# Scores of the first stretch over 128 rows: two k heads in one tile, each head's q beside zeros

## The chip, the core and the metric

The kernel runs on one core of a Trainium2 chip. Its engines are TensorE (PE; its weight loads stand apart as PEld), VectorE (DVE), ScalarE (ACT), GpSimd (POOL) and SyncE (SP, which issues every transfer of this kernel). Each engine takes its instructions strictly in its own order. The metric is the device time of one execution in microseconds, the median of several.

## What is computed

Attention over the 32 largest scores of each query, for 4 batches of 8 heads with 576 positions and head size 64, and then two MLPs on the 2304 tokens of 512 numbers.

```python
scores = scale * np.matmul(q, k.transpose(0, 1, 3, 2))
kth = np.partition(scores, -top_k, axis=-1)[..., -top_k:-top_k + 1]      # top_k = 32
scores = np.where(scores >= kth, scores, -1000000000.0)
attn = np.exp(scores - np.max(scores, axis=-1, keepdims=True))
attn = attn / (np.sum(attn, axis=-1, keepdims=True) + 1e-09)
x = np.matmul(attn, v)                    # then (tokens, 512)
h = x @ w_in;  x = (h - np.tanh(h)) @ w_out              # first MLP
h = x @ w_in2; out = np.where(h > 0.0, h, np.exp(np.minimum(h, 0.0)) - 1.0) @ w_out2
```

## The kernel before

The queries are cut into six chunks of 384. In each chunk the heads go in four pairs, and a pair's rows of scores form groups of at most three tiles of 128 queries by 576 keys. There are 48 groups, eight to a chunk. In chunk 0 (groups 0 to 7) and chunk 2 (groups 16 to 23) a group is one head's 384 queries.

A loop over "ticks" writes the program, four ticks to a group: loads at the start of a tick, then the top-32 search (`topk_steps`) with parts of MLP steps between its operations, then transposes of the exponentials (`transposed`), then `norm`, `attend` and `finish_pair`. The framework's scheduler then settles the order on each engine, with the tick order and a few priorities as its guide. So an edit in one place can move instructions elsewhere.

The search is DVE's: for each tile four times MAX8 (line 351: the eight largest) and three or four times MATCH_REPLACE8 (line 365: overwrite these) or, at the end, a masking operation (line 372, or ACT at lines 367 and 368).

Scores come in two ways. Most groups split q and k in high and low parts (`split_qk`) and multiply over 128 rows (lines 328 and 329). The groups of chunk 0 ("whole") and of chunk 2 ("parked") multiply unsplit float32 over the 64 rows of a head (line 326); the program's one matmul there is two MATMUL instructions in the profile. Each result of 128 by 288 is copied from PSUM by ACT (line 330). Whole scores (tile `ps`, three PSUM banks) go straight to the search. Parked ones (tile `pp`, two PSUM banks) are computed during the first stretch at low priority, copied to `sp`, stored to DRAM as `sd` (line 306), and read back much later. The first stretch is thus chunk 0's attention with chunk 2's scores beside it: 8 whole and 8 parked units, six score matmuls of the program each.

Loads of q and k are at lines 263 and 270. A whole or parked unit loads its head's q (64 rows by 384) into `qraw` and its head's k (64 rows by 576) into `kraw`, both in rows 0 to 63. There are two buffers each for whole units (tags `qraw`, `kraw`) and one each for parked units (tags `qp`, `kp`).

In the same stretch the MLP weights are prepared (`prepare`): a load of 512 KB (`wr`, line 166, three buffers), two ACT operations (lines 175 and 176, or 176 and 180), a product on POOL (line 178), a combination on DVE (line 181, output `wf`, two buffers), a split in high and low on ACT and POOL (lines 140 and 141, output `wp`), and a store to DRAM (line 186). Later chunks load the prepared weights (`wt`). MLP steps are `first` (matmul `h`, line 500), `gate`, and `second` (matmul `acc`, line 536). `attend` is the product with v (matmul `av`, line 415), `transposed` the transposes (`pt`, line 393).

Of the kernel before, what the change touches and what calls it, by code (L numbers as in the profile page):

```python
# [8 lines left out]
F32 = mybir.dt.float32  # L9
# [10 lines left out]
P = 128  # L20
B, H, S, D = 4, 8, 576, 64
# [4 lines left out]
HS = S // 2  # L26
# [51 lines left out]
QR_BUFS = 2  # L78
KR_BUFS = 2
# [19 lines left out]
NU = 384  # L99
# [8 lines left out]
def tile_topk_attention_two_mlps(  # L108
# [9 lines left out]
    nc = tc.nc  # L118

    def pool(name, bufs, space=None):  # L120
        kw = {} if space is None else {"space": space}
        return ctx.enter_context(tc.tile_pool(name=name, bufs=bufs, **kw))

    const = pool("const", 1)
    sb = pool("sb", 2)
# [10 lines left out]
    def f(ap):  # L136
        return ap.bitcast(F32)

    def split(hi, lo, src):
        nc.scalar.activation(hi, src, copy)  # L140
        nc.gpsimd.tensor_sub(lo, src, f(hi))  # L141

    def bank(tag, name, bufs):
        return ps.tile([P, 512], F32, tag=tag, name=name, bufs=bufs)
# [63 lines left out]
    for ci, size in enumerate(SIZES):  # L208
        for p in range(NPAIR):
            row = []  # L210
            c0 = 0
            for b, q0, n in CHUNKS[ci]:
                for heads in ([[0], [1]] if n >= 256 else [[0, 1]]):
                    u = Unit()
# [10 lines left out]
            cuts, k = [], 0  # L225
# [28 lines left out]
    def parked(u):  # L254

        return u.g.at in PARK

    def load_q(u):
        u.qraw = sb.tile([P, NU], F32, tag="qp" if parked(u) else "qraw", name=f"qraw{u.id}", bufs=1 if parked(u) else QR_BUFS)
        src = qT[u.b, 2 * u.p + u.heads[0] : 2 * u.p + u.heads[-1] + 1, :, u.q0 : u.q0 + u.n].rearrange("h d s -> d h s")  # L260
        nq = u.n * len(u.heads)
        for half in range(1 if u.whole or parked(u) else 2):
            nc.sync.dma_start(u.qraw[half * D : half * D + D, :nq].rearrange("d (h s) -> d h s", s=u.n), src)

    def load_k(u):
        u.kraw = {}
        for h in u.heads:
            u.kraw[h] = sb.tile([P, S], F32, tag="kp" if parked(u) else "kraw", name=f"kraw{u.id}_{h}", bufs=1 if parked(u) else KR_BUFS)
            for half in range(1 if u.whole or parked(u) else 2):
                nc.sync.dma_start(u.kraw[h][half * D : half * D + D], kT[u.b, 2 * u.p + h])  # L270

    def split_qk(u):

        if u.whole or parked(u):
            return
        u.kh, u.kl = {}, {}
        nq = u.n * len(u.heads)
        u.qs = sb.tile([P, NU], F32R, tag="qs", name=f"qs{u.id}", bufs=QS_BUFS)[:, :nq]
        nc.scalar.activation(u.qs, u.qraw[:, :nq], copy)
        nc.gpsimd.tensor_sub(u.qs[D:P], u.qraw[D:P, :nq], f(u.qs[D:P]))  # L280
        for h in u.heads:
            k = sb.tile([P, 2, S], F32R, tag="kk", name=f"kk{u.id}_{h}", bufs=KK_BUFS)
            u.kh[h], u.kl[h] = k[:, 0], k[:, 1]
            split(u.kh[h], u.kl[h], u.kraw[h])
# [7 lines left out]
    def segments(u, t):  # L292

        out = []
        for i, h in enumerate(u.heads):
            lo, hi = max(0, i * u.n - t * P), min(P, (i + 1) * u.n - t * P)
            if lo < hi:
                out.append((lo, hi, h, t * P + lo - i * u.n))
        return out

    def park(u, t):

        s = sb.tile([P, S], F32, tag="sp", name=f"sp{u.id}_{t}", bufs=PARK_BUFS)
        products(u, t, s, True)
        u.parked[t] = dr.tile([P, S], F32, tag=f"sd{u.id}_{t}", name=f"sd{u.id}_{t}")
        nc.sync.dma_start(u.parked[t], s)

    def scores(u, t):
        if t == 0:
            u.s = []  # L310
        s = sb.tile([P, S], F32, tag="s", name=f"s{u.id}_{t}", bufs=S_BUFS)
        u.s.append(s)
        if parked(u):
            nc.sync.dma_start(s, u.parked[t])
        else:
            products(u, t, s, u.whole)

    def products(u, t, s, whole):

        for half in range(2):  # L320
            cs = slice(half * HS, half * HS + HS)
            for lo, hi, h, _ in segments(u, t):
                pt = bank("h", f"pp{u.id}_{t}_{half}_{h}", 2) if parked(u) else bank("at", f"ps{u.id}_{t}_{half}_{h}", 3)
                qc = slice(t * P, t * P + P)
                if whole:
                    nc.tensor.matmul(pt[:, :HS], u.qraw[0:D, qc], u.kraw[h][0:D, cs], start=True, stop=True)  # L326
                else:
                    nc.tensor.matmul(pt[:, :HS], u.qs[:, qc], u.kh[h][:, cs], start=True, stop=False)  # L328
                    nc.tensor.matmul(pt[:, :HS], u.qs[:, qc], u.kl[h][:, cs], start=False, stop=True)  # L329
                nc.scalar.activation(s[lo:hi, cs], pt[lo:hi, :HS], copy)  # L330
# [283 lines left out]
    for g in groups:  # L614
        t0 = 4 * g.at
        for u in g.units:
            lead = 6 if u.whole else 8
            if parked(u):
                at = PARK_AT + PARK_STEP * parks[0]
                parks[0] += 1  # L620
                on(before, int(at) - 3, lambda u=u: (load_q(u), load_k(u)))
                for t in range(u.k):
                    on(ends, int(at + t * PARK_STEP / 3), lambda u=u, t=t: later(park, u, t))
            else:
                on(before, max(-6, t0 - lead) if u.whole else t0 - lead, lambda u=u: (load_q(u), load_k(u)))
                on(before, t0 - 5, lambda u=u: split_qk(u))
            on(before, t0 + (1 if hurried(u) else 3), lambda u=u: load_v(u))
        for blk in range(NB):
            if not hurried(g.units[-1]):
                on(late, t0 + 4 + (1 if g.units[0].ci == 1 else 0) + (0 if quick(g.units[-1]) else blk // 3), lambda g=g, blk=blk: transposed(g, blk))  # L630
        for j, (u, t) in enumerate(g.tiles):
            on(mid, t0 - 4 + j, lambda u=u, t=t: scores(u, t))
        for u in g.units:
            if hurried(u):
                continue
            if u.last:
                on(ends, t0 + (5 if quick(u) else 7), lambda u=u: norm(u.ci, u.p, u))
                on(ends, t0 + (5 if quick(u) else 7), lambda u=u: attend(u))
                on(ends, t0 + (5 if quick(u) else 7), lambda u=u: finish_pair(u))
# [93 lines left out]
```

## Time and profile before

| | us |
|---|---|
| median of 3 runs (1241.11, 1245.57, 1245.80) | 1245.57 |
| the profiled execution | 1243.85 |
| its span, from the first to the last instruction | 1242.1 |

| engine | busy us | share of the span |
|---|---|---|
| PE | 1191.5 | 96% |
| DVE | 975.6 | 79% |
| ACT | 773.8 | 62% |
| POOL | 583.8 | 47% |

The shares are means over stages that differ, so the rows below are taken by stretch. The profile lists the granted clock of PE as a share of full speed: 1.00 is 2.4 GHz, 0.50 is 1.2 GHz, and a number between is a mix of the two over the stretch. The share of the 16 DMA engines can come out a little above 1. A bracket at the end of a timeline row gives how long the engine sat idle before it, and what ended that.

### The profile page before, as it was taken

The numbers are of one execution on the slowest core, as the hardware profiler recorded it, in microseconds if no ns is written. First come the engines' busy times: TensorE is split into PE (matmuls) and PEld (weight loads), VectorE is DVE, ScalarE is ACT, GpSimd is POOL, SyncE is SP. The second block draws the span as 40 slices with busy tenths as digits, with TensorE's granted clock in tenths as the row PEclk, the third lists the DMA queues.
The fourth block names the chain that finished last, engine by engine and source line by source line (L and its number), as shares of the span: only waits on it lengthen the run. The fifth ranks groups of instructions, "written<-read, shape, count | busy, mean of one in ns | idle before, by whom it ended". The sixth has DMA issues, their size and how long they took to land.

```text
span 1242.1 us, 19800 instructions
## 1 busy us (share of the span) xinstructions
PE 1191.5 (96%) x6424; PEld 999.4 (80%) x6424; DVE 975.6 (79%) x1951; ACT 773.8 (62%) x1700; POOL 583.8 (47%) x613
## 2 busy tenths in 40 slices
PE   7799889999989999999999999999999999999998
PEld 4455569888768888988988989988988988889887
DVE  7989999999999999869889768899789997100111
ACT  5989988788786445556566565666555564432333
POOL 4676549978984232334433344544334413233221
PEclk9995689999999999999999999999999999999999
DMA  8999627897979875767756778768777655687672
GB/s 260 341 317 313 228 85 252 299 323 238 317 261 356 326 244 176 245 207 251 241 193 204 235 231 263 239 189 244 220 245 242 198 163 175 198 284 252 218 253 78
DMA packets 103080, 298.32 MB, mean 240 GB/s; under 512 B 12609, under 2 KB 27969, under 8 KB 102977
## 3 DMA queue, kind: packets, MB, share of 16 engines
q1 hardware_dynamic: 102976, 297.06, 72.9%
q8 instruction: 51, 0.84, 0.3%
q14 instruction: 53, 0.43, 0.1%
HBM read 251.66 MB, written 45.35 MB: 239 GB/s over the span
## 4 chain that ended last, share of the span: by engine, by line
PE 74%; DVE 8%; ACT 6%; DMA 6%; POOL 3%; issue 2%; SPq 1%; ACTq 0%; POOLq 0%; DVEq 0%
PE acc L536 28%; PE h L500 28%; PE av L415 5%; PE pt L393 5%; DMA wr<-in_w_dram 4%; DVE vm L351 3%; DVE w L365 2%; PE ps L328 2%; PE pp L326 2%; PE ps L329 2%; DMA kraw<-in_kT_dram 1%; DVE wf L181 1%; PE ps L326 1%; POOL wr L178 1%; ACT ph L394 1%
## 5 line engine op out<-in xcount | busy, mean ns | idle before, releaser
L141 POOL TENSOR_TENSOR gl<-g,gh 128x384 fp32r<-128x384 f32 x192 | 206.5, 1076 | 364.9 <-ACT gh L140 321.9
L351 DVE MAX8 vm<-w 128x8 f32<-128x576 f32 x432 | 316.0, 748 | 3.4
L536 PE MATMUL acc<-wt,gh 128*128 128x512 f32 x1008 | 268.3, 398 | 0.3 <-ACT gh L140 0.3
L536 PEld LDWEIGHTS acc<-wt,gh 128*128 128x128 f32 x1008 | 185.5, 188 | 34.5 <-issue 3.9
L365 DVE MATCH_REPLACE8 w<-vm,w 128x576 f32<-128x576 f32 x288 | 212.8, 740 | 0.0
L140 ACT ACTIVATE gh<-g 128x384 fp32r<-128x384 f32 x192 | 100.8, 525 | 82.9 <-DVE g L514 47.5
L500 PE MATMUL h<-zh,wt 128*128 128x384 f32 (+2 forms) x768 | 146.6, 326 | 2.3 <-ACT zh L555 1.9
L536 PE MATMUL acc<-wt,gl 128*128 128x512 f32 x504 | 148.2, 398 | 0.0
L514 DVE SCALAR_TENSOR_TENSOR g<-t,h 128x384 f32<-128x384 f32 x96 | 52.0, 542 | 118.7 <-ACT t L506 118.7
L351 DVE MAX8 vm<-s 128x8 f32<-128x576 f32 x144 | 107.2, 749 | 46.8 <-ACT s L330 46.5
L500 PE MATMUL h<-xh,wt 128*128 128x384 f32 x672 | 143.0, 340 | 0.0
L393 PE MATMUL pt<-ident,e 128*116 128x128 f32 (+1 forms) x720 | 119.0, 293 | 18.5 <-ACT s L330 6.1
L500 PEld LDWEIGHTS h<-zh,wt 128*128 128x128 f32 x768 | 124.9, 190 | 9.2 <-ACT zh L555 3.1
L330 ACT ACTIVATE s<-ps 128x288 f32<-128x288 f32 (+1 forms) x272 | 106.3, 412 | 41.1 <-PE ps L329 33.1
L394 ACT ACTIVATE ph<-pt 116x384 f32<-116x384 f32 (+1 forms) x240 | 110.6, 498 | 31.1 <-PE pt L393 30.0
L393 PEld LDWEIGHTS pt<-ident,e 128*116 128x116 f32 (+1 forms) x720 | 90.2, 143 | 45.6 <-ACT s L330 10.0
L500 PEld LDWEIGHTS h<-xh,wt 128*128 128x128 f32 x672 | 117.7, 188 | 6.9 <-issue 0.6
L372 DVE SCALAR_TENSOR_TENSOR e<-s,vm,e 128x576 f32<-128x576 f32 x115 | 113.3, 990 | 1.4 <-ACT e L355 0.6
L178 POOL TENSOR_TENSOR wr<-wr,tiny 128x512 f16<-128x512 f32 x64 | 92.1, 1443 | 41.9 <-ACT wr L176 38.7
L505 ACT ACTIVATE t<-h 128x384 f32<-128x384 f32 x96 | 46.7, 488 | 103.0 <-PE h L500 102.8
L536 PEld LDWEIGHTS acc<-wt,gl 128*128 128x128 f32 x504 | 92.7, 188 | 18.4 <-issue 0.6
L365 DVE MATCH_REPLACE8 w<-vm,s 128x576 f32<-128x576 f32 x144 | 106.6, 740 | 0.0
(83 smaller groups left out, 2029.9 us busy)
## 6 DMA issues: line engine op xcount, KB each, us to landing
wt<-w SPq DMA_DIRECT2D x336, 512.0 KB, 4.4
wr<-in_w_dram SPq DMA_DIRECT2D x64, 512.0 KB, 5.9
w<-wp SPq DMA_DIRECT2D x64, 512.0 KB, 4.9
kraw<-in_kT_dram SPq DMA_DIRECT2D x112, 144.0 KB, 4.3
vraw<-in_vL_dram SPq DMA_DIRECT2D x64, 160.0 KB, 2.9
qraw<-in_qT_dram SPq DMA_DIRECT2D x80, 96.0 KB, 3.9
sd<-sp SPq DMA_DIRECT2D x24, 288.0 KB, 4.7
s<-sd SPq DMA_DIRECT2D x24, 288.0 KB, 4.9
```

The lines of the kernel that those rows point to most:

```text
L140: nc.scalar.activation(hi, src, copy)
L141: nc.gpsimd.tensor_sub(lo, src, f(hi))
L178: nc.gpsimd.tensor_mul(top, scaled, tiny)
L330: nc.scalar.activation(s[lo:hi, cs], pt[lo:hi, :HS], copy)
L351: nc.vector.max(g.vm[:, j, min(r, 1)], u.s[t] if r == 0 else g.w[j])
L365: nc.vector.match_replace(g.w[j], v, u.s[t] if r == 0 else g.w[j], FILL)
L372: nc.vector.scalar_tensor_tensor(u.e[t], u.s[t], v[:, 7:8], u.e[t], op0=ALU.is_ge, op1=ALU.mult, accum_out=g.sum[:, j : j + 1])
L393: nc.tensor.transpose(pt[:kn, j * P : j * P + P], v.e[t][:, k0 : k0 + kn], ident)
L394: nc.scalar.activation(g.ph[:kn, blk, :nq], pt[:kn, :nq], copy)
L415: nc.tensor.matmul(banks[c0][h * D : h * D + D, : v.n], v.vraw[h][:kn, blk], v.g.ph[:kn, blk, cs], start=(blk == order[0]), stop=(blk == o ...
L500: nc.tensor.matmul(h[:, cs], wv[:, wi, kt], xs[:, kt, cs], start=(a == 0), stop=(a == len(jobs) - 1))
L536: nc.tensor.matmul(acc[ci, m][t], gx[:, t * P : t * P + P], wt[:, wi], start=(ft == 0 and k == 0), stop=(ft == NF - 1 and k == 2),)
```

## The change

For whole and parked units (`wide(u)`), a pair's k is one tile of 128 rows, head 0 in rows 0 to 63 and head 1 in rows 64 to 127. Both halves are loaded when head 0's unit comes up; head 1's unit loads no k. Each head's q keeps a tile of its own. It is loaded into the head's half of the rows, and POOL fills the other half with zeros. The score matmul then runs over all 128 rows, where the zeros take the other head out. Only group 0 keeps 64 rows. The tags and the number of buffers stay, so the two `kraw` buffers now hold two pairs instead of two heads.

```diff
+    pair_k = {}
+
+    def wide(u):
+
+        return u.whole or parked(u)
+
     def load_q(u):
-        u.qraw = sb.tile([P, NU], F32, tag="qp" if parked(u) else "qraw", name=f"qraw{u.id}", bufs=1 if parked(u) else QR_BUFS)
+        if wide(u):
+            h = u.heads[0]
+            tag, bufs = ("qp", 1) if parked(u) else ("qraw", QR_BUFS)
+            u.qraw = sb.tile([P, NU], F32, tag=tag, name=f"qw{u.id}", bufs=bufs)
+            nc.gpsimd.memset(u.qraw[(1 - h) * D : (2 - h) * D, : u.n], 0.0)
+            nc.sync.dma_start(u.qraw[h * D : h * D + D, : u.n], qT[u.b, 2 * u.p + h, :, u.q0 : u.q0 + u.n])
+            return
...
     def load_k(u):
+        if wide(u):
+            if u.heads[0] == 0:
+                tag, bufs = ("kp", 1) if parked(u) else ("kraw", KR_BUFS)
+                k = pair_k[u.ci, u.p] = sb.tile([P, S], F32, tag=tag, name=f"kw{u.id}", bufs=bufs)
+                for h in range(2):
+                    nc.sync.dma_start(k[h * D : h * D + D], kT[u.b, 2 * u.p + h])
+            u.kraw = pair_k[u.ci, u.p]
+            return
...
                 if whole:
-                    nc.tensor.matmul(pt[:, :HS], u.qraw[0:D, qc], u.kraw[h][0:D, cs], start=True, stop=True)
+                    rows = slice(0, D if u.g.at == 0 else P)
+                    nc.tensor.matmul(pt[:, :HS], u.qraw[rows, qc], u.kraw[rows, cs], start=True, stop=True)
```

The scheduler answers with another order on every engine, up to about row 840 of DVE's 1406; behind that DVE's and ACT's orders are the same as before. Two places matter below. In the names, `_0_1_192_1` is a parked unit (pair 0, batch 1, query 192 on, head 1), `_1_0_0_0` a whole one (pair 1, batch 0, head 0). The changed file's lines are 21 or 22 further down behind the edit (141, 166, 178 and 186 keep theirs).

POOL, from the first weights to the third, before:

```order
L178 TENSOR_TENSOR wr_13_0_505<-wr_13_0_505,tiny 128x512
L141 TENSOR_TENSOR wp_12_0_386<-wf_12_0_380,wp_12_0_386 128x512
L353 TENSOR_SCALAR mb_0_0_0_0_0_0_167<-vm_0_0_0_0_0_0_166 128x3
L141 TENSOR_TENSOR wp_12_1_398<-wf_12_1_392,wp_12_1_398 128x512
L178 TENSOR_TENSOR wr_13_1_517<-wr_13_1_517,tiny 128x512
```

and now, with what each waits for:

```order
L178 TENSOR_TENSOR wr_13_0_511<-wr_13_0_511,tiny 128x512 [waits DMAHW6_49,Activation_49]
L269 MEMSET qw_0_1_192_1_244 64x384 [waits PE_49]
L269 MEMSET qw_1_0_0_1_327 64x384 [waits PE_49]
L141 TENSOR_TENSOR wp_12_0_391<-wf_12_0_385,wp_12_0_391 128x512 [waits Activation_49]
L141 TENSOR_TENSOR wp_12_1_403<-wf_12_1_397,wp_12_1_403 128x512 [waits Activation_49]
L178 TENSOR_TENSOR wr_13_1_523<-wr_13_1_523,tiny 128x512 [waits DMAHW3_49,Activation_49]
```

Two fills, each waiting for PE to be done with the tile's last user, now stand ahead of `wp_12_0`. There are 16 such fills on POOL.

SP, the queue of transfers some 20 us into the run, before:

```order
L186 DMA w_12_1_98<-wp_12_1_398 128x1024
L166 DMA wr_14_1_640<-in_w_dram 128x512
L263 DMA qraw_0_1_192_1_239<-in_qT_dram 64x384
L270 DMA kraw_0_1_192_1_1_241<-in_kT_dram 64x576
L186 DMA w_13_0_99<-wp_13_0_513 128x1024
L306 DMA sd_0_1_192_0_2_347<-sp_0_1_192_0_2_340 128x576
L263 DMA qraw_1_0_0_1_323<-in_qT_dram 64x384
L270 DMA kraw_1_0_0_1_1_325<-in_kT_dram 64x576
```

and now:

```order
L270 DMA qw_0_1_192_1_244<-in_qT_dram 64x384
L270 DMA qw_1_0_0_1_327<-in_qT_dram 64x384
L284 DMA kw_2_0_0_0_490<-in_kT_dram 64x576 x2
L166 DMA wr_14_0_634<-in_w_dram 128x512
L186 DMA w_12_0_97<-wp_12_0_391 128x1024
L327 DMA sd_0_1_192_0_2_350<-sp_0_1_192_0_2_343 128x576
```

The loads of the second heads' k are gone here. The k that is loaded at this place is that of pair 2, a whole pair ahead of its use.

## Rows read from the trace of the kernel before

**Rows 1.** Busy time by stretch: PE, PEld, DVE, ACT, POOL, granted clock, DMA share.

```profile
0.00:40.00 40.00, 26.64 (x52) 16.15 (x52) 31.30 (x63) 25.07 (x53) 19.69 (x25) 1.00 0.86 291
40.00:160.00 120.00, 110.31 (x321) 63.35 (x322) 109.31 (x212) 110.00 (x255) 76.35 (x86) 0.76 0.84 286
160.00:380.00 220.00, 201.68 (x1199) 170.67 (x1198) 219.07 (x419) 183.03 (x392) 182.31 (x175) 0.96 0.77 256
380.00:520.00 140.00, 139.01 (x776) 119.97 (x775) 140.00 (x301) 70.20 (x152) 42.81 (x50) 1.00 0.78 272
520.00:1242.00 722.00, 713.88 (x4082) 629.27 (x4080) 475.94 (x960) 385.46 (x851) 262.60 (x277) 1.00 0.69 219
```

**Rows 2.** DVE's waits from 0 to 160: total us, times, longest.

```profile
DVE vm L351 <- ACT s L330: 11.4, 7, 5.7
DVE wf L181 <- POOL wr L178: 5.4, 4, 2.0
DVE wf L181 <- POOL wp L141: 0.4, 1, 0.4
```

**Rows 3.** The same view of windows, other stretches of the start.

```profile
10.00:20.00 10.00, 10.00 (x22) 6.84 (x22) 9.09 (x20) 7.68 (x18) 6.57 (x6) 1.00 0.82 275
20.00:120.00 100.00, 84.70 (x215) 47.47 (x215) 90.12 (x177) 88.84 (x204) 66.55 (x74) 0.84 0.95 328
70.00:80.00 10.00, 10.00 (x30) 5.40 (x31) 7.78 (x16) 10.00 (x24) 5.23 (x7) 1.00 0.92 292
90.00:120.00 30.00, 29.48 (x75) 16.91 (x75) 28.65 (x57) 28.18 (x68) 19.07 (x23) 0.50 0.95 328
```

**Rows 4.** Timeline of PE: start, us, line, tile, weights' rows*columns, moving rows x columns.

```profile
13.10 2.12 PE L326 MATMUL pp<-kraw,qraw 64*128 64x288 f32 x4
15.02 3.08 PE L326 MATMUL ps<-kraw,qraw 64*128 64x288 f32 x6
...
41.61 1.65 PE L393 MATMUL pt<-ident,e 128*116 128x128 f32 x6 [0.39 <-ACT e L368]
...
63.14 2.25 PE L326 MATMUL pp<-kraw,qraw 64*128 64x288 f32 x4 [1.85 <-DMA kraw<-in_kT_dram]
...
76.71 5.56 PE L415 MATMUL av<-ph,vraw 116*64 116x384 f32 x20
82.20 1.24 PE L326 MATMUL pp<-kraw,qraw 64*128 64x288 f32 x4
83.28 1.13 PE L326 MATMUL ps<-kraw,qraw 64*128 64x288 f32 x4
...
106.40 2.12 PE L326 MATMUL pp<-kraw,qraw 64*128 64x288 f32 x4
...
124.74 1.20 PE L393 MATMUL pt<-ident,e 128*116 128x128 f32 x9
```

**Rows 5.** Timeline of DVE: three waits for weights.

```profile
30.46 0.69 DVE L181 SCALAR_TENSOR_TENSOR wf<-sc,wr 128x512 uint32<-128x512 uint32 x1 [1.14 <-POOL wr L178]
68.46 0.69 DVE L181 SCALAR_TENSOR_TENSOR wf<-sc,wr 128x512 uint32<-128x512 uint32 x1 [1.36 <-POOL wr L178]
79.14 0.69 DVE L181 SCALAR_TENSOR_TENSOR wf<-sc,wr 128x512 uint32<-128x512 uint32 x1 [1.99 <-POOL wr L178]
```

**Rows 6.** Timeline of ACT: what stands behind the first two of these.

```profile
27.78 0.64 ACT L175 ACTIVATE sc<-wr 128x512 f32<-128x512 f32 x1 [1.89 <-DMA wr<-in_w_dram]
64.47 0.41 ACT L330 ACTIVATE sp<-pp 128x288 f32<-128x288 f32 x1 [0.95 <-PE pp L326]
```

**Rows 7.** Timeline of POOL: the nearest operations to a fill of 64x384.

```profile
0.71 0.20 POOL masks.py:197 MEMSET ident<- 128x128 f32 x1 [0.29 <-POOLq L721]
145.87 1.00 POOL L280 TENSOR_TENSOR qs<-qraw,qs 64x384 fp32r<-64x384 f32 x1 [1.10 <-ACT qs L279]
```

**Rows 8.** SP's waits from 0 to 160 before q loads: total us, times, longest.

```profile
SPq L263 <- PE pp L326: 5.1, 4, 2.3
SPq L263 <- PE ps L326: 4.5, 4, 1.4
```

More of the change, by code (lines that the diff above doesn't have):

```diff
@@ L256, in parked @@
         return u.g.at in PARK
+    pair_k = {}
+    def wide(u):
+        return u.whole or parked(u)
     def load_q(u):
-        u.qraw = sb.tile([P, NU], F32, tag="qp" if parked(u) else "qraw", name=f"qraw{u.id}", bufs=1 if parked(u) else QR_BUFS)
+        if wide(u):
[5 more added lines that the diff above has]
+            return
+        u.qraw = sb.tile([P, NU], F32, tag="qraw", name=f"qraw{u.id}", bufs=QR_BUFS)
         src = qT[u.b, 2 * u.p + u.heads[0] : 2 * u.p + u.heads[-1] + 1, :, u.q0 : u.q0 + u.n].rearrange("h d s -> d h s")
         nq = u.n * len(u.heads)
-        for half in range(1 if u.whole or parked(u) else 2):
+        for half in range(2):
             nc.sync.dma_start(u.qraw[half * D : half * D + D, :nq].rearrange("d (h s) -> d h s", s=u.n), src)
     def load_k(u):
+        if wide(u):
[6 more added lines that the diff above has]
+            return
         u.kraw = {}
         for h in u.heads:
-            u.kraw[h] = sb.tile([P, S], F32, tag="kp" if parked(u) else "kraw", name=f"kraw{u.id}_{h}", bufs=1 if parked(u) else KR_BUFS)
-            for half in range(1 if u.whole or parked(u) else 2):
+            u.kraw[h] = sb.tile([P, S], F32, tag="kraw", name=f"kraw{u.id}_{h}", bufs=KR_BUFS)
+            for half in range(2):
                 nc.sync.dma_start(u.kraw[h][half * D : half * D + D], kT[u.b, 2 * u.p + h])
     def split_qk(u):
-        if u.whole or parked(u):
+        if wide(u):
             return
```

## The prediction

> **What bounds the kernel now.** I read the windows by stretch first. From 380 us to the end PE is busy 852.89 of 862 us [rows 1]: whatever brings the point at 380 forward brings the end forward. From 160 to 380 DVE is busy 219.07 of 220 us while PE idles 18 [rows 1]: here the search and the preparation of weights on DVE set the pace, and since DVE never waits, the stretch has a fixed length. So the end moves by as much as DVE reaches 160 us earlier or later, and a gain in the first 160 us can be no more than DVE's idle time there. That time is small. From 40 to 160 DVE is idle 10.7 of 120 us [rows 1]. The list of its waits says for what [rows 2]: 11.4 us in seven waits for scores, of which 5.7 is the unavoidable first one, 5.4 us in four waits for POOL's product of a weight, and 0.4 us for a buffer. Behind the first wait this is 5.7 + 5.4 + 0.4 = 11.5 us, the ceiling of any gain. ACT is as full from 40 to 160 (110.0 of 120 us), and from 20 to 120 the DMA engines are 0.95 busy [rows 1, 3].
>
> PE looks busy in this stretch, and the timeline shows why. Four 64-row instructions follow one another in 15.02 - 13.10 = 1.92 us or, as a single row, 2.12 us: about 0.5 us each. At 82.20, right behind 20 `av` instructions, the next four start 1.08 us later, 0.27 us each [rows 4]. The same work takes half as long. The same holds for the transposes, 0.275 us each at 41.61 and 0.13 at 124.74 [rows 4]. From 90 to 120 the granted clock is 0.50, the lower level of 1.2 GHz [rows 3]. For the first 80 us the profile lists 1.00, but the durations there are those of the 0.50 stretch, so I go by the durations: PE runs the first stretch at the lower level, apart from some microseconds behind each `av`.
>
> What lifts it? PE was busy 10.00 of 10 us from 10 to 20 [rows 3] with 64-row matmuls, and the next ones were no faster. Then 5.56 us of `av`, which fill 116 rows, halved the time of what followed, and by 106.40 the 64-row matmuls were back at 0.5 us [rows 4]. The transposes at 124.74 stand behind the second `av`, with the same effect. That speaks for the rows filled, not for the time busy. The changed scores fill 128.
>
> **The change part by part.**
>
> *Score matmuls over 128 rows.* Their count stays: 16 units of 12 instructions, 192 in all. A 128-row one isn't in the trace in this form. The bounds are 0.27 us (64 rows, after `av`) and 0.5 us (64 rows, elsewhere) [rows 4]. The transposes, with 128 rows moving, take 0.13 us for 128 columns, 288/128 of which is 0.29 us [rows 4], so rows in themselves cost nothing. I take 0.27 us: the clock rises some microseconds behind group 0's twelve 64-row instructions and stays up. PE then has 192 x 0.23 = 44 us less to do in a stretch where DVE's idle time is the only thing that counts.
>
> The Trainium skill, page "TensorE: Matmul & The Clock Gate", Part 3 (packing small matmuls), says that a matmul over few rows takes the same time as one over all of them, and that the gain is to be had by placing two of them in different rows so that they run side by side. By that rule zeros beside a head's q give nothing and the change would end where rival B does; rows 4 agree about a single matmul at a given clock, and the rule leaves out what the clock does.
>
> *DVE's waits for scores*, 5.7 us in six places [rows 2]. Each is PE, then ACT's copy, then MAX8. With score matmuls at half the time, PE runs ahead as far as its three banks go. I take all 5.7.
>
> *DVE's waits for weights*, 5.4 us in four places [rows 2]. The one of 1.14 us at 30.46 goes back to a 512 KB load that landed at 27.78 [rows 5, 6]; PE has no part in it. The one of 1.36 at 68.46 stands behind ACT's copy at 64.47, which waited for `pp`, which waited at 63.14 for a head's k [rows 4 to 6]; with half the k waits gone and PE fast I take it, 1.4. The one of 1.99 at 79.14 has ACT ahead of it, busy 10.00 of 10 us from 70 to 80 [rows 3], and stays. The fourth (0.9) is at the start, and it stays too. So 1.4 of 5.4.
>
> *Fills on POOL*, 16 of 64x384. The trace has none; a fill of 128x128 took 0.20 us, and a product of 64x384 with two inputs 1.00 [rows 7]. By elements per row the first gives 0.6 us, which I take; 16 are 9.6 us (3.2 to 16). POOL has room, 76.35 of 120 us busy [rows 1]. But DVE does wait for POOL, 5.8 us [rows 2] for the 96 us that POOL works up to 160 [rows 1]; in that proportion 9.6 us more cost 0.6. Two of the fills now stand right ahead of the split that frees `wf` for DVE, so I take twice that, 1.2, as a loss, with ends 0 (every fill in a gap of POOL's) and 9.6 (rival C, where a fill also holds POOL while it waits for PE).
>
> *Loads.* The count stays, 16 of q and 16 of k. The two halves of k go ahead of the first weights, and the first DVE operation on weights comes some places later in DVE's order, which covers that, so I put zero; if it didn't, I would expect no more than the longest wait for a weight, 2.0 us [rows 2]. A whole pair's k comes a pair ahead, where before PE waited for a head's k with a single buffer. What that is worth is in the waits above.
>
> *The order.* The scheduler moves things up to about row 840 of DVE's 1406, by a few places either way. In the stretches where DVE or PE never idles, the order has little to give. I put zero and 2 us either way.
>
> Sum: 5.7 + 1.4 - 1.2 = 5.9 us gained. A check from transfers: at a share of 0.95 from 20 to 120 us, these 100 us cannot shrink by more than about 5 us before the engines are full [rows 3]; the slack behind 120 and the start have to give the rest. That fits the sum, and it says not to expect the ceiling of 11.5. From the profiled execution, 1243.85 - 5.9 = 1238.0 us. That execution is 1.7 us under the median of 1245.57, which is within the spread of those runs; I leave the sum where it is: 1238 us, 0.6% under the median.
>
> **The rivals.**
>
> *A: the clock rises, and ACT or the DMA engines take PE's place.* ACT is 92% busy and the transfers at 0.95 [rows 1, 3]; DVE's waits turn from "scores late" to "weights late". Only half of the 5.7 us for scores and none for weights is then won, less 1.2 for fills: 2.85 - 1.2, about 1.6 us, 1242.2. For it: 4 us of the weights' waits already have nothing to do with PE. Against it: the six waits for scores are 0.95 us on the mean, and ACT's copy takes 0.41 of it [rows 2, 6].
>
> *B: the clock doesn't rise.* Matmuls stay at 0.5 us: it was the dense `av` and not its rows, or zeros do not count as rows filled, or with PE at half its load the clock falls back between the bursts. Then k ahead of time wins the 1.4, and the fills cost 1.2: no change, 1243.7.
>
> *C: slower; POOL stands still behind its fills.* A fill cannot start before PE has read the tile's last content, and all of POOL's products and splits of weights stand behind it in order, then DVE's `wf`, which has two buffers. SP had this same wait before q loads: 5.1 + 4.5 = 9.6 us in eight places [rows 8]. If POOL inherits it and DVE meets it in full, with nothing won because PE stays slow, the time is 1243.85 + 9.6 + 1.2 = about 1255. It decides from the point where PE frees a tile later than POOL comes to the fill; a fast PE makes it rare.
>
> **How the numbers follow.** The forecast (clock up, waits for scores gone) has 0.50, A 0.24, B 0.14, C 0.12. The forecast's own range is from 1243.85 - 11.5 - 2 = 1230 to 1241. Adding A and B reaches to 1246, and the spread of the runs by another microsecond; C's far part is left out. Range 1230 to 1247. About 0.5% (6.2 us of 1245.57, so under 1239.3) is what a measurement of this kernel can tell from no change. Most of the forecast's case lies below that, A mostly not: faster 0.50, same 0.39, slower 0.11.
>
> **What would show it.** In the changed profile the 192 score instructions at about 0.27 us from some 15 us on, and transposes at 0.13; a granted clock near 1 from 90 to 120; DVE's waits for scores behind the first one under 2 us in total; DVE idle from 40 to 160 at about half of 10.7; the fills at about 0.6 us. The point from which PE never idles would come some 6 us sooner than 380. Wrong would be: score instructions still at 0.5 us (B), POOL's products waiting for PE by way of a fill (C), or waits for scores gone while DVE waits for weights as long as before or longer (A).

## The result: slower by 1.2%

The changed kernel takes 1259.84 us (median of 6 runs, 1256.26 to 1263.02) and the kernel before, on the same chip, 1245.43 (1240.52 to 1246.00). The ratio is 1.0116, with a 95% interval of 1.0098 to 1.0135. The forecast was 1238 with a range up to 1247. The profiled execution of the changed kernel takes 1256.26 us; its span is 1254.3.

The windows answer to [rows 1] (PE, PEld, DVE, ACT, POOL, granted clock, DMA share, GB/s):

```profile
0.00:40.00 40.00, 24.04 (x56) 14.92 (x56) 30.13 (x60) 22.49 (x49) 18.45 (x29) 0.82 0.78 259
40.00:160.00 120.00, 86.82 (x333) 50.94 (x332) 112.32 (x221) 114.68 (x266) 86.20 (x100) 0.80 0.86 297
160.00:380.00 220.00, 198.83 (x1164) 169.07 (x1164) 218.11 (x410) 176.56 (x376) 178.39 (x170) 0.95 0.74 250
380.00:520.00 140.00, 133.10 (x730) 113.94 (x731) 137.66 (x297) 69.89 (x150) 45.02 (x51) 0.98 0.74 260
520.00:1254.00 734.00, 726.11 (x4144) 639.77 (x4142) 482.48 (x967) 390.36 (x861) 266.10 (x281) 1.00 0.69 219
```

From 40 to 160 PE has 23 us less to do, and DVE does 3 us more work than before. The start has therefore become faster. The loss is behind it: from 160 to 520 PE is busy 331.9 us where it was 340.7, and executes 81 instructions fewer. DVE is as full as before from 160 to 380 (218.1 of 220, 1.8 us of waits), and all the same the end comes later. PE is the one that waits more. From 160 to 520 its waits ahead of the MLP's products (tiles `h` and `acc`) come to 16.4 us in 15 places, where they were 7.3 us in six. The largest before (total us, times, longest):

```profile
PE acc L536 <- ACT gh L140: 2.4, 2, 2.0
PE h L500 <- DVE g L519: 2.3, 1, 2.3
...
PE h L500 <- DVE g L514: 1.5, 1, 1.5
```

and in the changed kernel:

```profile
PE acc L558 <- ACT gh L140: 4.7, 2, 2.6
...
PE h L522 <- DVE g L536: 3.2, 2, 2.8
...
PE acc L558 <- POOL gl L141: 1.9, 3, 0.9
```

Here `g` is the gated hidden tile of an MLP step, and `gh` and `gl` are its high and low parts.

To see where, I followed one instruction of the MLP steps: the n-th `gh` on ACT. The first stands at 188.0 us in the profile of before. In the changed kernel it comes 3.7 us earlier, the 7th (215) is 2.3 late, the 10th (238) level, the 19th (302) 4.7 late, the 31st (380) 6.3 and the 49th (484) 13.5; from the 73rd (605) to the end the shift is 12 us. It wavers on the way and grows. The search doesn't follow: the first MAX8 of its 43 tiles from 183 to 490 us is between 3.0 us earlier and 5.0 later.

DVE's waits from 0 to 160 answer to [rows 2] (total us, times, longest):

```profile
DVE vm L373 <- ACT s L352: 10.0, 7, 5.6
DVE wf L181 <- POOL wp L141: 2.0, 1, 2.0
DVE wf L181 <- ACT wr L180: 1.5, 2, 1.1
DVE wf L181 <- POOL wr L178: 1.4, 2, 0.9
```

PE's timeline answers to [rows 4] (start, us, tile; the bracket is the idle time before the row, with what ended it):

```profile
14.87 1.53 PE L348 MATMUL pp<-kw,qw 128*128 128x288 f32 x4
...
17.69 1.13 PE L348 MATMUL pp<-kw,qw 128*128 128x288 f32 x4
...
22.59 3.81 PE L348 MATMUL pp<-kw,qw 128*128 128x288 f32 x8 [2.32 <-DMA qw<-in_qT_dram]
...
100.75 2.26 PE L348 MATMUL pp<-kw,qw 128*128 128x288 f32 x4 [2.03 <-DMA kw<-in_kT_dram]
...
107.16 1.13 PE L348 MATMUL pp<-kw,qw 128*128 128x288 f32 x4
```

The clock does rise: four score instructions take 1.13 us at 17.69, 0.28 each. Behind an idle PE they are back at 0.48 to 0.57 us (22.59, 100.75). The granted clock from 90 to 120 us is 0.85, where it was 0.50 [rows 3]:

```profile
90.00:120.00 30.00, 20.74 (x88) 12.99 (x88) 28.17 (x59) 28.07 (x68) 20.82 (x27) 0.85 0.95 318
```

### The profile page after: what moved, and what is told of

The parts are those of the page before. It is cut to its first block, busy times and chain, and to the rows that moved or that the text cites. A ratio compares the mean times of both kernels' runs of the same rounds, so it can differ in the third digit from the quotient of the medians.

```text
span 1254.3 us, 19826 instructions
## 1 busy us (share of the span) xinstructions
PE 1168.9 (93%) x6424; PEld 988.6 (79%) x6424; DVE 980.7 (78%) x1951; ACT 774.0 (62%) x1700; POOL 594.2 (47%) x629
## 4 chain that ended last, share of the span: by engine, by line
PE 69%; ACT 10%; DVE 10%; DMA 5%; issue 3%; POOL 3%; SPq 1%; ACTq 0%; POOLq 0%; DVEq 0%
PE h L522 28%; PE acc L558 28%; PE av L437 5%; PE pt L415 4%; DVE vm L373 4%; DVE w L387 3%; DMA wr<-in_w_dram 3%; PE ps L350 2%; DVE wf L181 2%; PE ps L351 2%; ACT s L352 1%; ACT wr L176 1%; ACT ph L416 1%; ACT e L390 1%; ACT e L377 1%
## 5 line engine op out<-in xcount | busy, mean ns | idle before, releaser
L522 PEld LDWEIGHTS h<-zh,wt 128*128 128x128 f32 x768 | 126.1, 191 | 10.7 <-ACT zh L577 3.9
L415 PE MATMUL pt<-ident,e 128*116 128x128 f32 (+1 forms) x720 | 116.4, 286 | 17.4 <-ACT e L390 8.1
L415 PEld LDWEIGHTS pt<-ident,e 128*116 128x116 f32 (+1 forms) x720 | 88.2, 140 | 39.9 <-ACT e L390 12.8
L527 ACT ACTIVATE t<-h 128x384 f32<-128x384 f32 x96 | 46.8, 489 | 109.0 <-PE h L522 109.0
L525 ACT ACTIVATE t<-h 128x384 f32<-128x384 f32 x96 | 47.1, 492 | 102.7 <-PE h L522 102.2
```

What stands on the lines that cost most here:

```text
L415: nc.tensor.transpose(pt[:kn, j * P : j * P + P], v.e[t][:, k0 : k0 + kn], ident)
L522: nc.tensor.matmul(h[:, cs], wv[:, wi, kt], xs[:, kt, cs], start=(a == 0), stop=(a == len(jobs) - 1))
```

## Two theories, and the crossing that tells them apart

Theory 1: the loss is the order in which the scheduler now puts the instructions of all engines behind 160 us. Theory 2: it is the edit's own work (fills that wait for PE, weights that come late, a clock that falls). Order and work can be crossed. A helper keeps each engine's instructions in a given order by edges that need no wait; the n-th instruction of the program text on an engine is the same in both kernels, apart from the loads of q and k and the fills, which are found by name.

**x1**: the changed work in the order of before.

```diff
+def pin(tc, order):
+    # keep each engine's instructions in a given order (edges without a wait)
...
+    for engine, tokens in order.items():
...
+        line = [plain[t] if isinstance(t, int) else known[t] for t in tokens if isinstance(t, int) or t in known]
+        for a, b in zip(line, line[1:]):
+            tc.add_manual_dep(b, a.name, info, reason="order")
...
         tile_topk_attention_two_mlps(tc, *args)
+        pin(tc, ORDER)
```

`ORDER` lists every engine as in the kernel before.

> The changed kernel (scores over 128 rows, fills, a pair's k in one tile) with the instructions of every engine kept in the order of the kernel before; only the fills lie where the scheduler puts them, and the second k half of a pair is issued right behind the first. Theory 1, the order: the loss lies in the order that the scheduler found for the work between 160 and 640 us, not in the edit's own work, so this kernel gains what the score stage gains, 1238 to 1246 us. Theory 2, the edit's own work (fills that wait for PE, later weights, the clock that falls back in PE's gaps): it stays at 1254 to 1262 us whatever the order.

**x2**: products over 64 rows in the order of the changed kernel, with a pair's k still in one tile.

```diff
-            nc.gpsimd.memset(u.qraw[(1 - h) * D : (2 - h) * D, : u.n], 0.0)
...
-                    rows = slice(0, D if u.g.at == 0 else P)
+                    rows = slice(h * D, h * D + D)
...
+        pin(tc, ORDER)
```

`ORDER` now lists every engine as in the changed kernel.

> The other half of the crossing: the order of the changed kernel on every engine, but the scores contract 64 rows per head as before (each head's q and k in its own half of the rows, no fills, a pair's k still in one tile). Theory 1, the order: 1254 to 1264 us, though no fill and no 128-row product is left in it. Theory 2, the edit's own work: 1243 to 1249 us.

Measured: x1 1242.16 us, ratio to before 0.9974 (0.9962 to 0.9985). x2 1260.43 us, ratio 1.0122 (1.0099 to 1.0145). Theory 1 holds and theory 2 falls. Without a fill and without a 128-row score product, the changed order costs what the changed kernel costs; with the whole edit and the old order, the kernel is faster than both.

The other corner of the crossing came later, with the fills as the work:

**fills_alone** is the kernel before with a fill of rows 64 to 127, which no product reads, in front of each of the 16 loads of q; **fills_in_order** is the same with the order of before held.

```diff
+            if u.whole or parked(u):
+                nc.gpsimd.memset(u.qraw[D:P, :nq], 0.0)
             nc.sync.dma_start(u.qraw[half * D : half * D + D, :nq].rearrange("d (h s) -> d h s", s=u.n), src)
```

> The kernel before with one part of the change alone: the 16 fills on POOL (of rows 64 to 127, which no product reads), one k tile per head and 64 rows per product as before, nothing held in order. The fills cost POOL 16 x 0.41 us; the scheduler moves only 27 of VectorE's instructions by 5 or more places (171 in the run pair_k, 181 in the changed kernel) and 837 of PE's. Theory 1, the order: near the kernel before, 1244 to 1252 us. Theory 2, the fills are what costs (they wait for PE, weights come late): 1252 to 1260 us.

> The run fills_alone (the kernel before with 16 fills on POOL, 1251.0 us) with every other instruction kept in the order of the kernel before. If the fills' own time and their waits for PE cost: 1249 to 1252 us again. If it was the order that the fills brought about: 1243 to 1246 us.

Measured: 1251.03 us, ratio 1.0055 (1.0038 to 1.0073), and with the order held 1244.23 us, ratio 1.0000 (0.9991 to 1.0010). Fills cost nothing that these runs can tell; the order that they bring about costs half a per cent. Nor does the holding itself cost anything. The profile of fills_in_order ends 2.8 us before that of the kernel before while the timed runs agree, so a shift of less than 3 us between two single profiles is no evidence here.

**pair_k**: the pair's k tile alone, 64 rows, no fills, nothing held (the diff of x2 without `pin`).

> One part of the change alone, with nothing held in order: a pair's two k heads in one tile, but 64 rows per product and no fills. The scheduler moves 171 of VectorE's and 1292 of PE's instructions by 5 or more places against the kernel before. Theory 1, the order: a time unlike the kernel before, 1250 to 1262 us if this order is of the kind of the changed kernel's. Theory 2, the edit's own work (fills, clock): 1244 to 1248 us, since neither is in it.

Measured: 1252.29 us, ratio 1.0062 (1.0047 to 1.0078), inside theory 1's range and outside theory 2's. Each of the two parts tried alone is slower with its own order; that the pair's k costs nothing in the old order is seen in x1, which has it.

## Where in the order

**h1** and **h2** join the two orders at the MLP's first step: the first piece from one kernel, the rest from the other, on all engines.

> The changed kernel with its own order up to the MLP's first step (the first 1526 instructions that the scheduler placed, 163 us in its trace) and the order of the kernel before for all that follows. Theory 1 with the loss placed behind 163 us: 1238 to 1246 us. Theory 1 with the loss placed in the first stretch (weights prepared late, a debt that shows only later): 1252 to 1262 us. Theory 2: 1254 to 1262 us.

> The opposite joint: the changed kernel with the order of the kernel before up to the MLP's first step (the first 1534 instructions, 166.5 us in the trace before), then the changed kernel's own order. Theory 1 with the loss placed behind 163 us: 1252 to 1262 us. Theory 1 with the loss placed in the first stretch: 1238 to 1246 us. Theory 2: 1254 to 1262 us.

Measured: h1 1250.65 us, ratio 1.0047 (1.0032 to 1.0062); h2 1258.36, 1.0104 (1.0073 to 1.0135). h2 is where theory 1 with the loss behind 163 us put it; h1 lies between its two ranges. Against x1, the changed order costs 1.3% behind the MLP's first step and 0.7% ahead of it. Most is behind, but h1 isn't as fast as x1, and in it the seam itself costs: its first `gh` comes 2.2 us late, where the changed kernel, with the same order up to 163 us, has it 3.7 us early.

**e_dve, e_pe, e_dve_pe**: the changed kernel with only some engines held in the old order, the others left to the scheduler. `ORDER` then lists DVE alone, PE alone, or these two.

> The changed kernel with VectorE alone kept in the order of the kernel before; PE, ACT, POOL and SP stand as the scheduler puts them around that (603 PE instructions and 262 of ACT still 5 or more places off). Theory 1a, it is VectorE's order that costs (the MLP's g, zl and wf stand 5 to 16 places later among the search's instructions at 260 to 400 us, each place 0.66 us): 1240 to 1247 us. Theory 1b, the orders of PE and ACT cost as much: 1250 to 1260 us.

> The changed kernel with PE alone kept in the order of the kernel before; the scheduler places the other engines around it and leaves 29 of VectorE's and 133 of ACT's instructions 5 or more places off. The run e_dve refuted that VectorE's order alone carries the loss. Theory 1b, PE's order carries it: 1240 to 1247 us. Theory 1c, it is the match of the engines' orders with each other, of which holding one does not give back much: 1250 to 1260 us.

> The changed kernel with PE and VectorE kept in the order of the kernel before, ACT, POOL and SP as the scheduler puts them (103 of ACT's instructions 5 or more places off). Theory 1b: 1240 to 1247 us, as in e_pe. Theory 1c: between e_dve (1259.6 us) and x1 (1242.2 us), 1244 to 1256 us, the rest lying with ACT, POOL or SP.

Measured: e_dve 1259.56 us, ratio 1.0110 (1.0090 to 1.0129); e_pe 1246.39, 1.0016 (1.0004 to 1.0029); e_dve_pe 1254.10, 1.0083 (1.0061 to 1.0106). My first guess, VectorE's order, falls: held alone it gives nothing back. Holding PE's order gives back most. But e_dve_pe, which holds it too, lies outside the range of theory 1b (PE's order carries the loss) and inside that of 1c (the engines' orders have to match each other). To place its loss: the shift of the first and of the 73rd `gh` against before, from the profiles (us, at 188 and 605) is:

| kernel | PE's order | 1st `gh` | 73rd `gh` | lost between |
|---|---|---|---|---|
| changed | new | -3.7 | +12.2 | 15.9 |
| x2 | new | -0.5 | +16.5 | 17.1 |
| h2 | new from 166 | -4.0 | +12.0 | 16.0 |
| e_dve | new | +4.0 | +18.4 | 14.4 |
| pair_k | new | +0.7 | +8.3 | 7.6 |
| fills_alone | new | +0.1 | +6.6 | 6.6 |
| h1 | old from 163 | +2.2 | +6.8 | 4.6 |
| x1 | old | -4.2 | -2.1 | 2.1 |
| e_pe | old | -1.8 | -0.6 | 1.2 |
| e_dve_pe | old | +8.0 | +10.2 | 2.2 |
| fills_in_order | old | -2.8 | -2.8 | -0.1 |

With PE in its old order throughout, 0 to 2 us are lost behind 188 in these runs; with PE in a new order 6.6 to 17 (and 5.8 in park_at_5, below). The loss of e_dve_pe lies ahead of 188. Its window from 0 to 160 shows DVE busy 135.7 us, where the changed kernel has 142.5:

```profile
0.00:160.00 160.00, 100.87 (x355) 62.27 (x355) 135.69 (x263) 131.49 (x301) 102.94 (x125) 0.82 0.84 286
```

and the list of DVE's waits there says why:

```profile
DVE wf L207 <- POOL wr L204: 10.8, 5, 3.9
```

DVE, held in its old order, stands still 10.8 us for weights that ACT and POOL, in an order of their own, prepare later (3.6 in x1). In e_dve this wait is 12.8 us, and it loses again between 160 and 260; its window there:

```profile
160.00:260.00 100.00, 85.64 (x472) 73.41 (x471) 94.87 (x177) 75.81 (x163) 70.71 (x72) 0.92 0.60 198
```

DVE's longest wait there is one for the MLP's tanh on ACT, whose order no longer matches DVE's:

```profile
DVE g L567 <- ACT t L551: 4.7, 1, 4.7
```

How one place costs is seen in PE's timeline of the changed kernel, around the first MLP steps:

```profile
183.25 2.93 PE L522 MATMUL h<-xh,wp 128*128 128x384 f32 x8 [1.46 <-DVE g L541]
...
210.17 2.92 PE L558 MATMUL acc<-wp,gh 128*128 128x512 f32 x6 [2.05 <-ACT gh L140]
```

and of x1, where the same work comes in the old order:

```profile
180.88 1.63 PE L548 MATMUL h<-xh,wp 128*128 128x384 f32 x8
...
205.09 0.96 PE L584 MATMUL acc<-wp,gl 128*128 128x512 f32 x3 [1.10 <-POOL gl L167]
...
208.87 1.56 PE L584 MATMUL acc<-wp,gh 128*128 128x512 f32 x6
```

In the new order PE comes to a product that can't start: at 183.25 DVE's `g` has yet to free the PSUM bank for `h`, at 210.17 `gh` isn't there. It idles 1.46 and 2.05 us, and then runs the next eight or six instructions at a granted clock of 0.50 and 0.51, 1.3 us more each time. Taken by themselves the two places come to 2.8 + 3.4 = 6.2 us; the shift goes from -3.7 to +2.3 between the first and the 7th `gh`. Some of it is made up by the 10th, so such a place shows how the order costs, and its price isn't lost in full.

**mlp_later, mlp_earlier**: x1 with the MLP's instructions on DVE (`g`, `zl`, `wf`) from 200 to 380 us moved by three search instructions. The edit is in the list for DVE alone: rows `g, s1, s2, s3` become `s1, s2, s3, g`, and the reverse.

> The kernel of run x1 (changed work in the order before, 1242.2 us) with one shift: the MLP's instructions on VectorE (g, zl, wf) that start at 200 to 380 us each stand 3 search instructions of 0.66 us later. Theory 1a, a place in VectorE's queue is paid as it stands: the MLP runs 2 us later and the end with it, 1243.5 to 1246 us. If the delays add up from step to step: 1250 us or more. If VectorE's order is not it: 1242 us.

> The same kernel with the opposite shift: the MLP's instructions on VectorE at 200 to 380 us each 3 search instructions earlier. Theory 1a: PE's idle time of 19 us between 160 and 380 us shrinks by some 2 us, 1239 to 1241.5 us, below both kernels. If the MLP's operands are not there so early VectorE stands still and the search comes late: 1243 to 1250 us. If VectorE's order is not it: 1242 us.

Measured: 1245.91 us, ratio 1.0007 (0.9996 to 1.0017), and 1246.96, 1.0009 (0.9997 to 1.0021). Against x1 both lose about 0.3%, 4 us. DVE's order does matter. mlp_later is at the upper end of its range. mlp_earlier doesn't beat both kernels but is in the range of the other case on record, that the operands aren't there so early: DVE idles 7.8 of the 220 us from 160 to 380, where it idles 0.9 in x1. Of the three places tried the old one is the fastest. These two hand-made shifts also lose 3.8 and 6.1 us behind 188 with PE's order kept, so PE's order is not the only one that can lose there.

**park_at_5, park_step_4, mlp_lift**: other orders of the same changed work, with nothing held. In the changed kernel the second MLP's steps of the first chunk stand up to 41 search instructions later on PE than before, and I took that for the loss.

```diff
-PARK_AT = 4
+PARK_AT = 5
```

```diff
-PARK_STEP = 3.5
+PARK_STEP = 4.0
```

```diff
+        with tc.high_priority(offset=20):
...
+            if todo and at_tick[tick][0] < 2 * NF:
+                a, b, c = (lambda f=f: lifted(f) for f in (a, b, c))
```

> The changed kernel with one number of its plan altered and nothing held: the first of the parked units comes one due tick later (5 in place of 4). The scheduler then puts the second MLP's steps of the first chunk on PE 0 to 22 search instructions earlier than the kernel before has them, where the changed kernel has them 0 to 41 later; 78 of VectorE's instructions stand 5 or more places off (181 in the changed kernel). If the search's instructions ahead of that MLP on PE are the loss: 1240 to 1248 us. If any order other than that of before costs as much: 1250 to 1260 us.

> The changed kernel with the parked units 4.0 ticks apart in place of 3.5, nothing held: on PE the second MLP's steps lie within 10 search instructions of the kernel before, but the first MLP's start 21 later and then 4 to 22 earlier; 172 of VectorE's instructions are 5 or more places off. If the second MLP's place on PE is the loss: 1240 to 1248 us. If the first MLP's or VectorE's order cost as much: 1250 to 1260 us.

> The changed kernel with the MLP steps of the first chunk raised by 20 in the scheduler's priority, nothing held: on PE the second MLP's steps come 2 to 36 search instructions earlier than in the kernel before, on VectorE 219 instructions stand 5 or more places off. If the search ahead of that MLP on PE is the loss: 1240 to 1248 us. If the search, now late itself, takes its place, or any other order costs: 1250 to 1260 us.

Measured: 1248.11 us, ratio 1.0032 (1.0020 to 1.0045); 1256.34, 1.0094 (1.0079 to 1.0109); 1260.36, 1.0129 (1.0113 to 1.0144). The place of that MLP alone isn't it: park_at_5 and mlp_lift both have it ahead of the old order, and one is the fastest of the three and the other the slowest. One number of the plan (park_at_5) gives back some 60% of what the order costs beside x1.

**own_166_290, own_from_290**: the order before, with the changed order in one piece of the stretch.

> The changed kernel with the order of the kernel before on every engine, but its own order for the middle piece, from the MLP's first step (166 us) to 290 us (PE's instructions 525 to about 1390). Reference points: x1, the order before throughout, 1242.2 us; h2, its own order from 166 us on, 1258.4 us. If the losses of the two halves add: the steps of h2 lie 6 to 7 us later at 302 us than at 215, so 1247 to 1250 us. If only the half behind 290 us counts, because VectorE has slack there to catch up: 1242 to 1245 us.

> The opposite: the order of the kernel before up to 290 us, the changed kernel's own order behind it. If the losses add: the steps of h2 lose another 9 us from 302 to 605, so 1250 to 1253 us. If only the half behind counts: 1255 to 1260 us, as in h2. If the half behind is harmless by itself: 1242 to 1245 us.

Measured: 1253.15 us, ratio 1.0064 (1.0046 to 1.0083), and 1254.73, 1.0078 (1.0060 to 1.0096). Against x1 that is 0.9% and 1.04%, each more than I expected if the halves added, and together more than h2's 1.3%. The costs don't add; each seam makes an order of its own.

So what is shown is that the orders carry the loss and the edit's work doesn't. That PE's order carries the part behind 188 us is not shown. The table speaks for it, but in e_pe the scheduler put the other engines near their old order as well (29 instructions on DVE and 133 on ACT stand five or more places off), no run gave PE alone the new order, and mlp_later and mlp_earlier lose there with PE's order kept. It may as well be how the engines' orders match; which moves do it stays open.

## Why the prediction was wrong

**The step that failed** is "The order": "In the stretches where DVE or PE never idles, the order has little to give. I put zero and 2 us either way." It is worth 1.4% with the changed work (1.0116 against 0.9974, some 18 us) and 1.2% with 64 rows (1.0122 against the kernel before, some 15 us). A full engine only says that it always had something to do. In the changed kernel DVE is busy 218.1 of 220 us from 160 to 380, while PE's waits ahead of the MLP's products go from 7.3 to 16.4 us (14.5 in x2, 8.6 in x1). That DVE sets the pace from 160 to 380 and that the stretch "has a fixed length" was read from one order, and I used it as a property of the stretch. "By a few places either way" was too small as well: the largest move is 25 places on DVE and 151 on PE.

**"The end moves by as much as DVE reaches 160 us earlier"** holds only roughly with the order kept: fills_in_order is 2.8 us early at 188 and 2.8 at the end, x1 4.2 and 2.1, and differences under 3 us between single profiles are no evidence. With the new order the sign turns, from -3.7 to +12.2.

**Sizes, with the order kept** (x1; DVE's waits from 0 to 160):

```profile
DVE vm L399 <- ACT s L378: 7.4, 4, 5.5
DVE wf L207 <- POOL wr L204: 3.6, 4, 1.6
DVE wf L207 <- DMA qw<-in_qT_dram: 1.7, 1, 1.7
...
DVE wf L207 <- POOL wp L167: 0.4, 1, 0.4
```

- Waits for scores behind the first: 1.9 us, forecast under 2, so 3.8 of the 5.7 were won. In the changed kernel 4.4 are left. DVE is idle 6.0 us from 40 to 160, near the half of 10.7 that was forecast.
- Waits for weights: 3.6 + 1.7 + 0.4 = 5.7 us, as against 5.8 [rows 2]. The 1.4 us put there weren't won. The wait at 68.46 fell from 1.36 to 0.80 us (67.70 below), but the first one rose from 0.9 to 1.59. The one at 79.14 stayed, as forecast (1.69 at 78.07). The view puts it down to a load of q, but POOL's product of the weight ends just ahead of it, at 76.70 + 1.35 = 78.05:

```profile
14.34 0.69 DVE L207 SCALAR_TENSOR_TENSOR wf<-sc,wr 128x512 uint32<-128x512 uint32 x1 [1.59 <-POOL wr L204]
...
67.70 0.69 DVE L207 SCALAR_TENSOR_TENSOR wf<-sc,wr 128x512 uint32<-128x512 uint32 x1 [0.80 <-POOL wr L204]
...
76.70 1.35 POOL L204 TENSOR_TENSOR wr<-wr,tiny 128x512 f16<-128x512 f32 x1 [1.09 <-ACT wr L202]
...
78.07 0.69 DVE L207 SCALAR_TENSOR_TENSOR wf<-sc,wr 128x512 uint32<-128x512 uint32 x1 [1.69 <-DMA qw<-in_qT_dram]
```

- Fills: they cost nothing (fills_in_order), where I put 1.2 us. One takes 0.42 us instead of 0.6:

```profile
L269 POOL MEMSET qw<- 64x384 f32 x16 | 6.5, 416 | 14.7 <-PE ps L348 12.1 <-issue 1.5 <-PE pp L348 0.7
```

- The sum is then 3.8 + 0.1 - 0 = 3.9 us instead of 5.9, and x1 measures 3.2 (0.26%, interval 1.9 to 4.7).

**The clock** rose as foreseen, but not for good: from 90 to 120 us, where the forecast had it near 1, it was 0.85, and 0.72 in x1. The 192 score instructions of the changed kernel take 38.9 + 31.9 + 6.5 = 77.3 us of PE time, 0.40 each, where the forecast had 0.27. Rival B had this, "with PE at half its load the clock falls back between the bursts", at 0.14, and the forecast's own case took 0.27 throughout:

```profile
L348 PE MATMUL pp<-kw,qw 128*128 128x288 f32 x96 | 38.9, 537 | 23.7 <-ACT sp L352 8.8 <-DMA kw<-in_kT_dram 7.8 <-DMA qw<-in_qT_dram 5.3
L348 PE MATMUL ps<-kw,qw 128*128 128x288 f32 x84 | 31.9, 506 | 8.2 <-ACT s L352 4.2 <-ACT ph L416 3.8
...
L348 PE MATMUL ps<-kw,qw 64*128 64x288 f32 x12 | 6.5, 706 | 4.3 <-DMA kw<-in_kT_dram 4.3
```

That the products over 128 rows are faster is not the order's doing: in x2 the 192 products over 64 rows, in the same order, take 97.2 us, 0.51 each:

```profile
L373 PE MATMUL pp<-kw,qw 64*128 64x288 f32 x96 | 49.2, 651 | 21.2 <-ACT sp L377 9.8 <-DMA kw<-in_kT_dram 6.1 <-issue 1.7
L373 PE MATMUL ps<-kw,qw 64*128 64x288 f32 x96 | 48.0, 672 | 10.5 <-DMA kw<-in_kT_dram 4.2 <-ACT s L377 3.3 <-ACT ph L441 2.8
```

The Trainium skill, page "TensorE: Matmul & The Clock Gate", Part 3, says that a product over few rows leaves most of the array idle. By that rule, as the prediction weighed it, the zeros would have given nothing. At one level of the clock the traces agree with it: four score products take 1.13 us over 128 rows (17.69 above) and over 64 ([rows 4], at 83.28). The measured 0.26% speak for the gain by the clock, though x1 also has the pair's k a pair ahead, and no run parted the two.

**Rival C** is there in the trace and isn't the cause. POOL waits for PE ahead of a fill, 12.1 us in three places, of which 10.3 at one fill at the start:

```profile
POOL qw L269 <- PE ps L348: 12.1, 3, 10.3
```

But x2 has no fill and is as slow, and fills_in_order has sixteen and is as fast as before. It gave the right sign for a wrong reason.

**The range** ended at 1247 because the only slower case was C, at 0.12. That a worse order could cost more than the edit can gain was no rival, although the prediction saw moves up to row 840 of DVE's 1406. Counted, 181 of 1404 instructions on DVE and 1538 of 5944 on PE stand five or more places off.

## A version that beats both

x1, the change with the old order held, is at 0.9974 (0.9962 to 0.9985) of the kernel before and about 1.4% under the changed kernel. Here the gain is real, and smaller than what it sets in motion. Its windows are those of before [rows 1] but for PE's lighter start:

```profile
40.00:160.00 120.00, 88.91 (x340) 53.05 (x340) 113.98 (x224) 114.22 (x267) 82.19 (x97) 0.79 0.82 287
...
160.00:380.00 220.00, 201.31 (x1188) 172.26 (x1189) 219.08 (x414) 180.60 (x383) 181.30 (x175) 0.95 0.77 260
```

## What to carry to other kernels

Where a scheduler sets the order, an edit has two effects, its work and the order that follows from it; hold the old order and time the new work in it, and the reverse, before explaining anything. A stretch in which an engine never idles is not a stretch of fixed length: ask whether its work is due, and who is waiting meanwhile. If the differences in order are larger than the edit, give them a share of the forecast with the width that such differences have shown, here 0.3 to 1.6% against x1 (mlp_later, mlp_lift).

## What the chip showed beside

- An idle time of PE can cost more than itself. Behind 1.46 us and 2.05 us in the changed kernel the next products ran at the lower level of the clock (2.93 us for eight that take 1.63, 2.92 for six that take 1.56). Its length alone doesn't decide: behind 2.00 us in x1 six such products took 1.66 us at a granted clock of 1.00. The windows of the two places in the changed kernel:

```profile
183.25:186.00 2.75, 2.75 (x9) 2.75 (x10) 2.75 (x7) 2.37 (x6) 2.75 (x4) 0.50 0.76 311
210.17:213.00 2.83, 2.83 (x7) 2.14 (x8) 2.83 (x7) 2.78 (x6) 2.68 (x4) 0.51 0.71 221
```

and in x1 the window and the row of PE's timeline:

```profile
374.90:376.50 1.60, 1.56 (x7) 1.25 (x8) 1.60 (x5) 1.60 (x4) 1.34 (x2) 1.00 0.55 174
...
374.94 1.66 PE L584 MATMUL acc<-wp,gh 128*128 128x512 f32 x6 [2.00 <-ACT gh L166]
```

- A fill of 64x384 on POOL takes 0.42 us, the 128x128 one took 0.20 [rows 7].
